# Two attention branches change places, and the first unit is prepared partly inside the branch

## The chip, the cores and the metric

The kernel runs on one core of one Trainium2 chip. The metric is the device time of one execution in microseconds; the number that counts is the median of several runs.

## The reference

Sliding-window attention with sink keys, then a mixture of eight experts whose gate is balanced in 8 rounds of row and column scaling, then one more layer. Everything is float32 in the reference; the last layer's weights come as float64.

```python
# attention: q, k, v are (2, 8, 768, 64); n_sink = 4, window = 128
scores = q @ k.T / sqrt(D)
keep = (key < n_sink) | ((0 <= query - key) & (query - key < window))
a = softmax(where(keep, scores, -1e9))          # + 1e-09 in the denominator
x = (a @ v) as (1536, 512)                      # heads side by side
# mixture: w_gate (512, 8), w1 (8, 512, 1024), w2 (8, 1024, 512)
P = exp(x @ w_gate - max)
for _ in range(8):
    P /= P.sum(1) + 1e-9;  P /= P.sum(0) + 1e-9;  P *= N / E
x = sum over e of P[:, e] * (relu(x @ w1[e]) @ w2[e])
# last layer: w_in (512, 2048), w_out (2048, 512)
h = x @ w_in
out = (h - tanh(h)) @ w_out
```

n_sink and window are inputs of the run, not constants.

## The kernel before

The order of all work is written out by hand (the scheduler is set to manual), so each engine does its instructions in the order in which the code issues them. Products run on float32 values that are split into a high and a low part (`split`, `split_hi`: ACT casts the high part at L58 or L63, DVE subtracts it at L59 or L64 to get the low one), three products for one.

`run` first issues the loads of the keys and queries of units 0 and 1 (`load_unit`, L198, on SP's queue). A unit is two heads of one batch, so there are 8 units, each with 6 tiles of 128 queries. Then it builds the mask material: `far` and `col` on POOL, finished on DVE from the two run-time numbers, `flag_i` (L134: 1 where n_sink is at most 32 and window is between 1 and 128) and three bias tiles: `b0` (L142) for the first tile of queries, `b1` (L160, L161, and a memset) for the second, `b2` (L164 to L166) for the others. SP then issues the loads of the first four weight pieces (`stage_next`, L517, 512 KB each).

Behind that come the first products. `keep_busy` (L187) issues products of zeros that nothing reads, in order to keep PE's clock up. `prep` prepares a third of a unit: four transposes on PE (L209) into one PSUM bank, the casts on ACT (L63) into `kT` and `qT`, and then the subtractions on DVE (L64); it is a generator with three steps, so the caller decides what lies between them. For unit 0, third `part` has the tiles 2*part and 2*part + 1 of keys and of queries. For third 0 POOL also copies the sink keys into their slots (L224). Before the branch all three thirds of unit 0 are prepared, in three PSUM banks of their own, with 8, 4 and 4 zero products between them; `b1` and `b2` are made on DVE in between.

Then every engine reads the flag into a register and branches. If the flag is 1, `attention_narrow` runs; otherwise `attention_any`, a longer program for any window, which is compiled into the kernel but not run with these inputs. The arms lie in memory in the order in which the code has them: code up to the branch, the arm for a true condition, the arm of `Else`, the code behind the join.

`attention_narrow` is a loop over 48 steps t (unit u, tile i) and five more to drain it. Step t issues, in this order: scores of tile t on PE (`qk`, L267); on DVE the bias with the maximum (`soft1`, `araw`, L284), together with the end of the sums of step t - 1 (L278, L289); in the first three steps four zero products; the scaling of the probabilities of step t - 1 on DVE (`soft3`, L306); what earlier steps left in the list `later` (above all DVE subtractions, L64); in the odd tiles the four transposes of a third of the next unit into pool `ps_t`; the transposes of the probabilities of step t - 2 (`a_transpose`, L320 and L325), also into `ps_t`, with a copy on ACT; the exponentials on ACT (`soft2`, L297); then the casts of the third, whose subtractions are put into `later`; and the products with v of step t - 3 (`pv`, L356, from tile 1 on). `ps_t` has two buffers of one PSUM bank each.

Behind the join `moe` runs: `g1` (L662) and `g2` (L669) are the products of the experts and of the last layer, and the gate's steps lie among the first of them.

## Time and profile before

| | |
|---|---|
| median of 3 runs | 1465.67 us |
| fastest run | 1465.48 us |
| span of the profiled execution, first to last instruction | 1464.2 us |
| PE busy with products | 1443.6 us, 99% of the span |
| DVE, ACT, POOL busy | 864.4, 451.3, 141.7 us |
| chain that ended last: PE, DVE, "issue", ACT | 82%, 12%, 3%, 3% |
| last attention product ends | 122.3 us after the span's start |

The span leaves out what lies around the first and the last instruction, 1.5 us against the median. The chain that ended last is followed back from the last instruction to whatever released it; "issue" in it is time in which the engine waited for nothing that the profile shows. A product's end is modelled, so durations of neighbouring products overlap; the distance between their starts is the better measure.

### The profile page before, as it was taken

What the parts mean: (1) busy time and instruction counts of PE and PEld (TensorE: products, weight loads), DVE (VectorE), ACT (ScalarE), POOL (GpSimd) and SP (SyncE); (2) the same over time, 40 slices, a digit from 0 to 9 for tenths busy, and PEclk for the clock granted to TensorE, in tenths of its full rate; (3) what the DMA queues carried; (4) which work ended last, traced back from release to release, by engine and by line L of the source; (5) the groups of instructions that cost most, each with busy time, mean ns of one, the idle gap of its engine ahead of it and who ended that gap; (6) DMA issues with size and microseconds to landing.
All of it is one profiled execution on the core that took longest, in us unless ns stands there. A gap on an engine that the chain in (4) does not pass through costs nothing.

```text
span 1464.2 us, 17440 instructions
## 1 busy us (share of the span) xinstructions
PE 1443.6 (99%) x6731; PEld 1171.0 (80%) x6731; DVE 864.4 (59%) x1810; ACT 451.3 (31%) x864; POOL 141.7 (10%) x127
## 2 busy tenths in 40 slices
PE   8999999999999999999999999999999999998998
PEld 6666888888888888888888888888888878787887
DVE  6893233466356446625653563465352289999997
ACT  6994212200211210022112102210211256665553
POOL 1110000000000000000000000000000135346431
PEclk9999999999999999999999999999999999999999
DMA  7341000321121031112112211221220011000011
GB/s 166 84 125 37 29 1 12 106 66 48 49 96 52 28 101 65 58 41 93 54 37 86 79 53 34 94 65 36 73 76 4 23 36 43 15 30 29 0 44 44
DMA packets 91674, 81.05 MB, mean 55 GB/s; under 512 B 42816, under 2 KB 71744, under 8 KB 91584
## 3 DMA queue, kind: packets, MB, share of 16 engines
q1 hardware_dynamic: 91296, 79.86, 18.0%
q8 instruction: 55, 0.90, 0.2%
q14 instruction: 35, 0.29, 0.1%
q10 hardware_dynamic: 288, 0.00, 0.0%
HBM read 68.31 MB, written 11.53 MB: 55 GB/s over the span
## 4 chain that ended last, share of the span: by engine, by line
PE 82%; DVE 12%; issue 3%; ACT 3%; DMA 0%; POOL 0%; SPq 0%; DVEq 0%; ACTq 0%
PE p L662 40%; PE p L669 39%; DVE y L764 3%; ACT an L297 2%; DVE mk L758 1%; DVE y L761 1%; DVE y L759 1%; DVE y L763 1%; DVE araw L284 1%; DVE an L306 1%; PE pt L325 1%; DVE kT L64 0%; PE pg L609 0%; PE sc L267 0%; ACT at L326 0%
## 5 line engine op out<-in xcount | busy, mean ns | idle before, releaser
L669 PE MATMUL p<-w2p,h 128*128 128x512 f32 x2880 | 669.1, 390 | 8.2 <-ACT h L769 4.9
L669 PEld LDWEIGHTS p<-w2p,h 128*128 128x128 f32 x2880 | 539.3, 188 | 122.8 <-POOL h L770 5.2
L662 PE MATMUL p<-xh,w1p 128*128 128x512 f32 x1920 | 608.5, 392 | 2.2 <-issue 2.2
L662 PEld LDWEIGHTS p<-xh,w1p 128*128 128x128 f32 x1920 | 362.6, 189 | 78.3 <-issue 3.1
L662 PE MATMUL p<-xl,w1p 128*128 128x512 f32 x960 | 375.4, 391 | 0.0
L694 ACT ACTIVATE h<-p 128x512 fp32r<-128x512 f32 x192 | 114.8, 598 | 791.9 <-PE p L662 787.4
L695 DVE SCALAR_TENSOR_TENSOR h<-p,h 128x512 fp32r<-128x512 f32 x192 | 132.5, 690 | 259.6 <-ACT h L694 259.3
L662 PEld LDWEIGHTS p<-xl,w1p 128*128 128x128 f32 x960 | 181.4, 189 | 37.5
L683 DVE SCALAR_TENSOR_TENSOR acc<-p,prob,acc 128x512 f32<-128x512 f32 x84 | 63.0, 750 | 206.1 <-PE p L669 206.1
L59 POOL TENSOR_TENSOR w1p<-stage,w1p 128x1024 fp32r<-128x1024 f32 x8 | 22.0, 2747 | 1041.3 <-ACT w1p L58 1041.3
L770 POOL TENSOR_TENSOR h<-y,h 128x512 fp32r<-128x512 f32 x47 | 81.6, 1735 | 145.4 <-DVE th L762 141.9
L764 DVE COPY_PREDICATED y<-mk,th 128x512 f32<-128x512 uint8 x48 | 84.1, 1751 | 1.7
L760 ACT ACTIVATE tq<-tq,kst 128x512 f32<-128x512 f32 x48 | 34.8, 725 | 78.1 <-DVE y L759 78.1
L297 ACT ACTIVATE an<-araw,nmax 128x288 f32<-128x288 f32 (+1 forms) x96 | 48.7, 514 | 2.7 <-DVE nmax L284 2.1
L758 DVE TENSOR_SCALAR mk<-tq 128x512 uint8<-128x512 f32 x48 | 43.1, 898 | 2.1 <-ACT tq L755 2.1
L59 DVE TENSOR_TENSOR w2p<-stage,w2p 128x1024 fp32r<-128x1024 f32 x32 | 39.2, 1225 | 7.9 <-ACT w2p L58 7.9
L58 ACT CAST w2p<-stage 128x1024 fp32r<-128x1024 f32 x40 | 41.7, 1043 | 0.0
L284 DVE CUSTOM_DVE_ANT_0 araw<-sc,bias 128x288 f32<-128x288 f32 (+1 forms) x96 | 39.7, 414 | 0.0
L267 PE MATMUL sc<-kT,qT 64*128 64x288 f32 (+1 forms) x288 | 36.9, 330 | 0.4 <-DVE qT L64 0.3
L755 ACT ACTIVATE tq<-p 128x512 f32<-128x512 f32 x48 | 28.7, 597 | 27.2 <-PE p L662 27.2
L267 PEld LDWEIGHTS sc<-kT,qT 64*128 64x128 f32 x288 | 23.4, 185 | 15.3 <-issue 14.6
L58 ACT CAST w1p<-stage 128x1024 fp32r<-128x1024 f32 x36 | 35.6, 1047 | 0.0
(129 smaller groups left out, 953.9 us busy)
## 6 DMA issues: line engine op xcount, KB each, us to landing
stage<-in_moe_w_dram SPq DMA_DIRECT2D x64, 512.0 KB, 3.5
n<-in_moe_w_in_dram SPq DMA_DIRECT2D x32, 256.0 KB, 2.8
n<-in_moe_w_out_dram SPq DMA_DIRECT2D x32, 256.0 KB, 2.7
wf_in<-n SPq DMA_DIRECT2D x32, 128.0 KB, 1.7
wf_out<-n SPq DMA_DIRECT2D x32, 128.0 KB, 1.7
stage<-wf_in SPq DMA_DIRECT2D x8, 512.0 KB, 3.2
stage<-wf_out SPq DMA_DIRECT2D x8, 512.0 KB, 3.6
v<-in_v_dram SPq DMA_DIRECT2D x16, 192.0 KB, 2.5
```

What stands on the lines that cost most here:

```text
L58: self.nc.scalar.copy(out=hi, in_=src)
L59: (engine or self.nc.vector).tensor_tensor(out=lo, in0=src, in1=hi.bitcast(F32), op=ALU.subtract)
L267: nc.tensor.matmul(sc[t][h][:, :n], lhsT=self.qT[u % 2][rows, zq, i * P : (i + 1) * P], rhs=self.kT[u % 2][rows, zk, c0 : c0 + n], start=m ...
L297: nc.scalar.activation(out=an[t][:, h, :n], in_=araw[t][:, h, :n], func=AF.Exp, bias=nmax[t][:, h : h + 1], scale=-1.0, accum_out=ssum[t][ ...
L662: nc.tensor.matmul(ps, lhsT=wt[:, zw, kk, cols], rhs=xx[:, kk, tok], start=m == 0, stop=m == 3 * KD - 1)
L669: nc.tensor.matmul(ps, lhsT=ht[:, zh, n * P : (n + 1) * P], rhs=ws[j // 2][:, zw, j % 2, :], start=start and m == 0, stop=stop and m == last,)
L683: V.scalar_tensor_tensor(out=acc[n], in0=ps, scalar=prob[:, n, e : e + 1], in1=acc[n], op0=ALU.mult, op1=ALU.add)
L694: nc.scalar.activation(out=h[j][:, 0], in_=ps, func=AF.Relu)
L695: V.scalar_tensor_tensor(out=h[j][:, 1], in0=ps, scalar=0.0, in1=h[j][:, 0].bitcast(F32), op0=ALU.max, op1=ALU.subtract)
L758: V.tensor_scalar(out=mk, in0=tq, scalar1=TAN_T2, scalar2=None, op0=ALU.is_ge)
L764: V.copy_predicated(y, mk, th)
L770: engine.tensor_tensor(out=ht[:, 1], in0=y, in1=ht[:, 0].bitcast(F32), op=ALU.subtract)
```

## The change

The condition of the branch is turned round: the arm for `flag == 0` comes first and is `attention_any`, the `Else` arm is `attention_narrow`. Before the branch only third 0 of unit 0 is prepared, with 8 and 4 zero products, in 2 PSUM banks instead of 4. The other two thirds are prepared in steps 0 and 2 of the loop of `attention_narrow`, in `ps_t`; `b1` is made in step 0 and `b2` in step 1. The rest of the diff takes out comments and docstrings.

```diff
+            self.far, self.col = far, col
             with ExitStack() as early:
-                pools = [early.enter_context(tc.tile_pool(name=f"ps_w{i}", bufs=1, space=PSUM)) for i in range(4)]
+                pools = [early.enter_context(tc.tile_pool(name=f"ps_w{i}", bufs=1, space=PSUM)) for i in range(2)]
                 busy = pools[0].tile([P, 512], F32, name="busy")
-                first = [self.prep(0, part, pools[1 + part], "m") for part in range(3)]
+                first = self.prep(0, 0, pools[1], "m")
                 self.keep_busy(busy, 8)
-                next(first[0])
+                next(first)
                 self.keep_busy(busy, 4)
-                next(first[1])
-                next(first[0])
-                next(first[0])
-                self.keep_busy(busy, 4)
-                next(first[2])
-                V.tensor_tensor(out=b1[:, :P], in0=far[:, 0], in1=col, op=ALU.max)
-                V.tensor_copy(out=b1[:, TW:], in_=far[:, 1])
-                for part in (1, 1, 2, 2):
-                    next(first[part])
-                V.tensor_copy(out=b2[:, :P], in_=far[:, 0])
-                V.tensor_copy(out=b2[:, P:TW], in_=col[:, :SK])
-                V.tensor_copy(out=b2[:, TW:], in_=far[:, 1])
+                next(first)
+                next(first)
...
-            with tc.If(flag == 1) as cond:
+            with tc.If(flag == 0) as cond:
                 with ExitStack() as c1:
-                    self.attention_narrow(c1)
+                    self.attention_any(c1)
             with cond.Else():
                 with ExitStack() as c2:
-                    self.attention_any(c2)
+                    self.attention_narrow(c2)
...
             if t <= T:
                 soft1(t)
+            if t == 0:
+                b0, b1, b2 = self.bias
+                nc.vector.tensor_tensor(out=b1[:, :P], in0=self.far[:, 0], in1=self.col, op=ALU.max)
+                nc.vector.tensor_copy(out=b1[:, TW:], in_=self.far[:, 1])
+            elif t == 1:
+                nc.vector.tensor_copy(out=b2[:, :P], in_=self.far[:, 0])
+                nc.vector.tensor_copy(out=b2[:, P:TW], in_=self.col[:, :SK])
+                nc.vector.tensor_copy(out=b2[:, TW:], in_=self.far[:, 1])
             if t < 3:
                 self.keep_busy(ps_k.tile([P, 512], F32, tag="k", name=self.nm("busy")), 4)
...
             if t < T and u + 1 < units and i % 2 == 1:
                 pr = self.prep(u + 1, i // 2, ps_t, "t")
                 next(pr)
+            elif t in (0, 2):
+                pr = self.prep(0, 1 + t // 2, ps_t, "t")
+                next(pr)
```

## Rows read from the trace of the kernel before

**Rows 1.** Chain of waits over the whole span: start us, us, what.

```profile
by line: PE p L662 39.8%; PE p L669 39.1%; DVE y L764 2.9%; issue 2.8%; ACT an L297 1.6%; DVE mk L758 1.3%; DVE y L761 1.3%; DVE y L759 1.2%; DVE y L763 1.2%; DVE araw L284 0.8%; DVE an L306 0.7%; PE pt L325 0.7%; DVE kT L64 0.4%; PE pg L60
...
179.18 5.49 PE p L662 x24
```

**Rows 2.** Chain of waits, 110 to 160 us, at the join.

```profile
122.36 2.22 issue
124.58 8.56 PE p L662 x24
```

**Rows 3.** Windows at the join: length, engines' busy time, PEclk, DMA share, GB/s.

```profile
122.40:123.80 1.40, 0.00 (x0) 0.00 (x0) 0.69 (x1) 0.57 (x1) 0.60 (x3) 1.00 0.15 14
...
124.58:130.60 6.02, 6.02 (x14) 4.78 (x15) 0.19 (x1) 0.71 (x2) 0.00 (x0) 0.50 0.02 5
```

**Rows 4.** Timeline at the join: start us, us, instruction, [idle before, releaser].

```profile
121.22 1.12 PE L368 MATMUL px<-ats,vS 64*128 64x512 f32 x2
...
123.00 0.69 DVE L64 TENSOR_TENSOR xl<-px,xh 128x512 fp32r<-128x512 f32 x1 [3.59 <-ACT xh L63]
...
125.95 0.19 DVE L59 TENSOR_TENSOR wgs<-wg,wgs 128x32 fp32r<-128x32 f32 x1 [2.26 <-ACT wgs L58]
```

**Rows 5.** DMA queues, 121 to 126 us: packets, MB, share of 16 engines.

```profile
q8 instruction: 2, 0.03, 2.4%
q14 instruction: 3, 0.02, 1.8%
```

**Rows 6.** Timeline up to the branch, 0 to 12 us.

```profile
6.04 1.17 PE L187 MATMUL busy<-idle 128*128 128x512 f32 x4
6.28 0.16 DVE L134 TENSOR_TENSOR flag_i<-ok 128x1 int32<-128x1 f32 x1
7.48 0.41 DVE L64 TENSOR_TENSOR qT<-m,qT 128x256 fp32r<-128x256 f32 x1
8.27 0.34 POOL L245 MEMSET vS<- 64x128 f32 x2 [0.33 <-issue]
8.29 0.41 PE L209 MATMUL m<-ident,raw_q 128*128 128x128 f32 x2 [0.78 <-DMA raw_q<-in_q_dram]
```

**Rows 7.** DMA queues, 0 to 15 us.

```profile
q1 hardware_dynamic: 7861, 3.10, 88.9%
```

**Rows 8.** Timeline of the first attention steps, PE and DVE.

```profile
10.32 0.55 PE L267 MATMUL sc<-kT,qT 64*128 64x128 f32 x6 [0.25 <-DVE qT L64]
13.23 0.46 DVE L284 CUSTOM_DVE_ANT_0 araw<-sc,bias 128x288 f32<-128x288 f32 x1
13.78 0.60 PE L209 MATMUL m<-ident,raw_k 128*128 128x128 f32 x4
14.06 0.47 DVE L306 TENSOR_SCALAR an<-an,ssum 128x128 f32<-128x128 f32 x2
14.31 0.67 PE L267 MATMUL sc<-kT,qT 64*128 64x288 f32 x6
15.01 0.46 DVE L284 CUSTOM_DVE_ANT_0 araw<-sc,bias 128x288 f32<-128x288 f32 x1
16.40 0.68 DVE L64 TENSOR_TENSOR kT<-m,kT 128x512 fp32r<-128x512 f32 x1
17.34 0.60 PE L325 MATMUL pt<-ident,an 128*128 128x128 f32 x4
17.88 0.45 DVE L284 CUSTOM_DVE_ANT_0 araw<-sc,bias 128x288 f32<-128x288 f32 x1
19.71 0.45 DVE L284 CUSTOM_DVE_ANT_0 araw<-sc,bias 128x288 f32<-128x288 f32 x1
21.89 0.66 PE L325 MATMUL pt<-ident,an 128*128 128x128 f32 x4 [0.29 <-DVE qT L64]
```

**Rows 9.** Windows on DVE, subtractions of a third, then the last bias tile.

```profile
10.79:11.46 0.67, 0.67 (x3) 1.00 1.11 303
11.46:11.90 0.44, 0.44 (x5) 1.00 1.11 340
```

## The prediction

> **What bounds the kernel now.** I read the chain of waits first. Its summary by line gives 39.8% of the span to the products of L662 alone, and a stretch of them at full speed looks like 24 products in 5.49 us [rows 1]; once these products run, little else ends last. A change ahead of them is therefore worth what it moves their start. That start is set by the attention stage and by one hole behind it: the last attention product ends, the chain shows 2.22 us of "issue" (PE waits for nothing that the profile knows of), and the next 24 products take 8.56 us instead of 5.49 [rows 2]. [...] So the join of the two branches costs 2.22 + 3.07 = 5.3 us today.

> What the hole is shows in the timeline there. PE starts its last attention group at 121.22 and the next product at 124.58, 3.36 later; DVE starts its last attention subtraction at 123.00 and its next instruction at 125.95, 2.95 later [rows 4]. Pauses of about 3 us on both, at different moments, are hardly one engine waiting for another. In the same five microseconds the instruction queues move 2 and 3 packets [rows 5]: the engines jump from the end of the short-window arm over the whole any-window arm, and the code behind it has to be fetched. At the start there is no such jump: the arm that runs is the one that lies next, and POOL's idle time at that branch is 0.33 us [rows 6], the price of reading the flag and falling through.

> **The change, part by part.**

> *The join.* The short-window arm now lies last, next to the code that follows, so its end needs no far jump. Removed: the 2.22 us (0.1 us is left, for a short branch) and, if PE goes on without a hole, the slow clock behind it, 8.56 - 5.49 = 3.07 us [rows 1, 2]. Gain 5.2 us. Its bounds are 2.1 (the clock falls all the same, since the last attention steps are thin) and 5.3.

> *The branch.* The far jump is now at the start, over the any-window arm. By the loops of that arm PE skips 2 x (48 + 6 x 116) = 1488 products, each with its weight load; DVE and ACT skip some hundreds of instructions, SP and POOL a few dozen. The price of such a jump lies between PE's hole of 2.22 and 3.36 us; I take DVE's 2.95, as that instruction stands alone and is timed from its start [rows 2, 4]. When do the engines jump? The flag is written at 6.28 + 0.16 = 6.44. PE's four zero products of 6.04 end at 7.21 [rows 6]; with 0.5 us to read the flag (POOL's 0.33, rounded up) PE jumps at 6.95, while they still run, and goes on at 9.9. DVE's last subtraction of the first third starts at 7.48 [rows 6]; with the flag it jumps at 8.0 and goes on at 10.95. But the loads of this time take 88.9% of the DMA engines over the first 15 us [rows 7], where the join had them nearly idle. I add 0.3 us (bounds: 0, and 3, a doubling): **PE at 10.2, DVE at 11.2**. Before, the first scores started at 10.32 [rows 8].

> [...]

> If SP paid 3 us too, its first load of v would start that much later, but v is first read in step 4 of the loop, which itself moves by more.

> *What the pause takes the place of.* Until 10.32 PE prepared the other two thirds (the last queries landed at 8.29 [rows 6]), ACT cast them, DVE subtracted and made two bias tiles. Ahead of the branch go away 8 transposes, 4 zero products, 4 casts, 4 subtractions and 5 bias instructions. All but the zero products come back inside the loop; no DMA moves. The bias tile of step 0 costs nothing: DVE makes it while PE does that step's zero products. What costs is 0.67 us for two subtractions of a third and 0.44 for the bias tile of step 1 [rows 9].

> *PE's clock.* PE idles from 7.21 to 10.2. At the join the clock fell 1.4 us into such a hole and came back after 6.0 us of products [rows 3]. I take the same: half speed from 10.2 to about 16.2. Bound below: no fall.

> *The first steps* (durations from [rows 8]). From 10.2 at half speed: first scores 1.0 us (0.55 at full), four zero products 1.7 (0.43 each, 14 in 6.02 us [rows 3]), four transposes of the second third 1.1, the second scores 1.3 up to the first head. DVE's second pair of araw starts at **15.3** instead of 13.23, +2.1. At full clock the same line gives 13.1, -0.1. From araw DVE needs 14.06 + 0.47 - 13.23 = 1.30 us to the end of the scaling, then the new 1.11 us of bias and subtractions, on which the third scores wait; from scores to araw it is 15.01 - 14.31 = 0.70, and 0.1 for the event. So 3.2 us instead of 1.78: araw of step 2 comes **+3.5** late.

> *A wait that is new.* In the loop the thirds live in ps_t, two banks that the transposes of the probabilities use too. Units are prepared in odd steps, so that in the next step one bank stays free; now preparations run in steps 0, 1, 2 and 3. A preparation's bank comes free with its subtractions, which DVE does a step later. In step 2 the new third holds one bank, and the probabilities' transposes need the other, which DVE frees at the end of its own step 2; in step 3 it is the same. PE's next scores are queued behind these transposes, DVE's next araw waits for the scores. (The wait exists today with a step's slack: the transposes of 21.89 wait 0.29 us for DVE [rows 8].) Step 2 to 3: araw and scaling 16.40 - 15.01 = 1.39, subtraction 0.68, two transposes 0.4, scores 0.67, events 0.1: 3.25 instead of 17.88 - 15.01 = 2.87, +0.4. Step 3 to 4: 1.39 + 0.67 + 0.60 + 0.67 + 0.1 = 3.4 instead of 19.71 - 17.88 = 1.83, +1.6. From there the steps are the old ones. **Loss 5.5 us**; below that 1.35 (full clock, another bank), above it what the fetch takes more.

> **Sum.** 5.5 lost at the start, 5.2 won at the join: +0.3. The profiled span of 1464.2 becomes 1464.5; with the 1.5 us between that span and the median of the runs, 1466.0.

> **The rivals.**

> A. The above: two effects of one size. 1466.0, by itself 1465.0 to 1467.5. Chance 0.44.

> B. The clock holds at the start, since PE was busy up to the hole, while the join's hole came after thin work. Loss 5.5 - 2.15 = 3.35, net -1.85: 1463.8. Against it: 3 us idle, twice what the clock bore at the join. 0.17.

> C. Slower: the code is fetched among the loads and takes 6 us instead of 3. All behind it moves by 3 us more: net +3.3, 1469.0. From a fetch of 3 us on the change loses. For it: the 88.9%; against it: code has a queue of its own. 0.13.

> D. Slower, since the change doesn't do what it says: the hole at the join isn't the far jump, or a fetch comes there anyway. Nothing is won, 5.5 lost: 1471.2. Against it: PE and DVE pause at different times for one length. 0.09.

> E. The banks cost nothing, as ACT is what steps 2 to 4 wait for anyway. Loss 3.5, net -1.7: 1464.0. 0.13. Together with B: loss 1.35, net -3.85, 1461.8, 0.04.

> **How the numbers follow.** The forecast is A. 1462.3 to 1469.6 holds A, B, C and E (0.87) and leaves out D and the pair of B and E. 2% is 29 us, about what a measurement of this kernel can tell from no change; the largest case, D, is 5.5 us, and 2% would need a fetch of over 30 us. So faster 0.01, same 0.98, slower 0.01.

> **What would show it.** At the join: the first L662 product within 0.3 us of the last attention product, the clock at 1.00, 24 products in 5.5 us; a gap of 2 us there is D. At the start: a packet on an instruction queue before 10 us; PE idle from 7.2 to about 10.2, a much later end being C; the granted clock of 10 to 16 us at 0.50, and 1.00 being B. In the loop: transposes of steps 2 and 3 that wait for DVE's subtractions, the first araw of step 4 near 25.2 instead of 19.71, and the last attention group near 121.2 + 5.5 = 126.7; without these waits it is E. The forecast is wrong altogether if the products from the join to the end don't take the time they took before.

## The result

The changed kernel takes 1472.64 us (median, 1472.17 to 1474.54), the kernel before 1465.62 us beside it. Single runs far outside the rest (1595.86 us for the kernel before, 2403.75 for the loop alone below) are left out of all ratios. The ratio is 1.0052, with a 95% interval of 1.0037 to 1.0067: slower, clear of noise, though far within 2%. The forecast was 1466.0 in a range of 1462.3 to 1469.6. The span of the profiled execution is 1470.6 us instead of 1464.2, so 6.4 us have to be found.

The page of the changed kernel counts lines of its own file: its scores are L258, its transposes of the probabilities L311 and L316, its expert products L664 and L671.

The join did what was forecast. The chain of waits of the changed kernel, 118 to 165 us (start us, us, what; to be compared with [rows 2]), and the start of the last attention group in the timeline (to be compared with [rows 4]):

```profile
132.61 1.05 PE px L359 x2
133.66 5.67 PE p L664 x24
...
132.54 1.12 PE L359 MATMUL px<-ats,vS 64*128 64x512 f32 x2
```

There is no hole any more, and 24 products take 5.67 us instead of 8.56. From the start of the last attention group (121.22 before [rows 4], 132.54 now) to the end of these products it was 124.58 + 8.56 - 121.22 = 11.92 us [rows 2, 4] and is 133.66 + 5.67 - 132.54 = 6.79: 5.1 won, against 5.2 forecast.

But that last group starts 11.3 us later than before, where 5.5 were forecast. 11.3 - 5.1 = 6.2 is the loss of the span but for 0.2 us. All of the error lies at the start. The chain of waits there, 0 to 40 us:

```profile
7.33 4.64 issue
11.96 0.91 PE sc L258 x6
12.87 2.00 PE busy L178 x4
14.87 0.85 PE m L200 x4
15.73 0.78 PE sc L258 x3
16.50 0.92 issue
17.43 0.45 PE sc L258 x3
```

PE is without work for 4.64 us at the branch, and then a second time for 0.92, in the middle of the second scores: three of their six products are done, the next three wait for nothing that the profile knows of. The instruction queues, 6 to 10 us:

```profile
q8 instruction: 1, 0.02, 2.0%
q14 instruction: 2, 0.02, 1.4%
```

So code is fetched at the start now, among the loads (225 GB/s from 6.0 to 9.6 us); before, neither queue has a packet in the first 15 us. In windows of 0.1 us the packet on q8 comes at 9.0, 2.9 us before PE goes on, and its next at 15.1, 2.3 us before PE goes on again. What follows in the loop shows the timeline of the first steps (start us, us, instruction, [idle before, releaser]; to be compared with [rows 8]):

```profile
17.96 0.46 DVE L275 CUSTOM_DVE_ANT_0 araw<-sc,bias 128x288 f32<-128x288 f32 x1 [3.48 <-PE sc L258]
...
20.77 0.46 DVE L275 CUSTOM_DVE_ANT_0 araw<-sc,bias 128x288 f32<-128x288 f32 x1 [0.27 <-PE sc L258]
...
22.98 0.41 PE L311 MATMUL pt<-ident,an 128*128 128x128 f32 x2 [0.69 <-DVE kT L64]
...
23.43 0.37 ACT L312 COPY at<-pt 128x256 f32<-128x256 f32 x1 [3.36 <-PE pt L311]
23.70 0.54 ACT L288 ACTIVATE an<-araw,nmax 128x288 f32<-128x288 f32 x1
...
24.87 0.17 DVE L269 TENSOR_SCALAR ssum<-ssum 128x2 f32<-128x2 f32 x1 [2.04 <-ACT an L288]
24.95 0.45 DVE L275 CUSTOM_DVE_ANT_0 araw<-sc,bias 128x288 f32<-128x288 f32 x1
...
27.13 1.12 PE L316 MATMUL pt<-ident,an 128*128 128x128 f32 x4 [2.57 <-DVE qT L64]
...
29.95 0.17 DVE L269 TENSOR_SCALAR ssum<-ssum 128x2 f32<-128x2 f32 x1 [2.87 <-ACT an L288]
30.02 0.45 DVE L275 CUSTOM_DVE_ANT_0 araw<-sc,bias 128x288 f32<-128x288 f32 x1
```

Here the wait for the banks is in the trace as forecast: the transposes of steps 2 and 3 wait for DVE's subtractions (0.69 and 2.57 us). What the reader should see beside it is ACT: its copy of the transposed probabilities starts at 23.43, and the exponentials of the step, whose input DVE had finished at 21.7, come behind that copy in ACT's order. DVE then waits 2.04 us for them, and in the next step 2.87 us in the same way. The windows of PE (length, busy, granted clock, DMA share, GB/s):

```profile
9.60:16.20 6.60, 4.24 (x17) 0.50 1.04 311
16.40:26.60 10.20, 6.29 (x38) 1.00 0.79 178
26.80:33.40 6.60, 6.27 (x29) 0.50 0.00 1
33.60:40.00 6.40, 6.40 (x59) 1.00 0.01 3
```

PE's clock falls twice: in the hole, as forecast, and again at about 26.7, in the 2.57 us in which PE waits for DVE. The four transposes behind that wait take 1.12 us, not 0.60.

The start of the first araw of a step, from the DVE timelines of all these kernels, gives the account by steps (us; the loop alone from its second run):

| step | before | changed | swap only | loop only | own bank |
|---|---|---|---|---|---|
| 1 | 13.23 | 17.96 | 23.54 | 10.84 | 18.43 |
| 2 | 15.01 | 20.77 | 26.40 | 13.65 | 21.82 |
| 3 | 17.88 | 24.95 | 29.27 | 17.84 | 25.12 |
| 4 | 19.71 | 30.02 | 31.11 | 22.91 | 27.73 |
| 7 | 26.36 | 37.74 | 37.75 | 31.43 | 35.80 |

Changed against before: 4.73 late at step 1, then 1.03, 1.31 and 3.24 more in the next three steps, 1.07 more up to step 7, together 11.38. Behind that the distance stays.

### The profile page after: what moved, and what is told of

Its sections match the earlier page's. It is cut to its first block, busy times and chain, and to the rows that moved or that the text cites. A ratio compares the mean times of both kernels' runs of the same rounds, so it can differ in the third digit from the quotient of the medians.

```text
span 1470.6 us, 17424 instructions
## 1 busy us (share of the span) xinstructions
PE 1445.0 (98%) x6727; PEld 1171.7 (80%) x6727; DVE 865.2 (59%) x1810; ACT 450.9 (31%) x864; POOL 141.6 (10%) x127
## 4 chain that ended last, share of the span: by engine, by line
PE 83%; DVE 11%; issue 3%; ACT 2%; POOL 0%; DVEq 0%; ACTq 0%
PE p L664 39%; PE p L671 39%; DVE y L766 3%; ACT an L288 1%; DVE y L763 1%; DVE mk L760 1%; DVE y L765 1%; DVE y L761 1%; PE pt L316 1%; DVE araw L275 1%; PE sc L258 1%; DVE an L297 1%; PE px L347 1%; PE m L200 1%; PE busy L178 0%
## 5 line engine op out<-in xcount | busy, mean ns | idle before, releaser
L671 PE MATMUL p<-w2p,h 128*128 128x512 f32 x2880 | 669.4, 390 | 8.5 <-ACT h L771 4.8
L671 PEld LDWEIGHTS p<-w2p,h 128*128 128x128 f32 x2880 | 539.5, 188 | 122.8 <-POOL h L772 5.3
L664 PE MATMUL p<-xh,w1p 128*128 128x512 f32 x1920 | 606.1, 390 | 0.0
L664 PEld LDWEIGHTS p<-xh,w1p 128*128 128x128 f32 x1920 | 361.2, 188 | 75.4 <-issue 0.8
L664 PE MATMUL p<-xl,w1p 128*128 128x512 f32 x960 | 374.0, 390 | 0.0
L664 PEld LDWEIGHTS p<-xl,w1p 128*128 128x128 f32 x960 | 180.6, 188 | 37.2
L258 PE MATMUL sc<-kT,qT 64*128 64x288 f32 (+1 forms) x288 | 38.5, 343 | 5.8 <-issue 5.6
L258 PEld LDWEIGHTS sc<-kT,qT 64*128 64x128 f32 x288 | 24.4, 195 | 21.9 <-issue 21.2
```

The lines of the kernel that those rows point to most:

```text
L258: nc.tensor.matmul(sc[t][h][:, :n], lhsT=self.qT[u % 2][rows, zq, i * P : (i + 1) * P], rhs=self.kT[u % 2][rows, zk, c0 : c0 + n], start=m ...
L664: nc.tensor.matmul(ps, lhsT=wt[:, zw, kk, cols], rhs=xx[:, kk, tok], start=m == 0, stop=m == 3 * KD - 1)
L671: nc.tensor.matmul(ps, lhsT=ht[:, zh, n * P : (n + 1) * P], rhs=ws[j // 2][:, zw, j % 2, :], start=start and m == 0, stop=stop and m == last,)
```

## The experiments

Theory T, formed from these rows: the start loses by code that is fetched among the loads, by a second packet of code that is fetched right behind the first, and by the waits in steps 2 to 4, with the second fall of the clock. Rival R: all of it is the fetch of code, that of DVE and ACT included, and the banks cost nothing.

**The swap alone and the loop alone.** The two halves of the change, each by itself. The swap alone, in the kernel before:

```diff
-            with tc.If(flag == 1) as cond:
+            with tc.If(flag == 0) as cond:
                 with ExitStack() as c1:
-                    self.attention_narrow(c1)
+                    self.attention_any(c1)
```

(and the other arm in the Else). The loop alone is the changed kernel with these lines put back.

> The arms change places, but all three thirds and the bias tiles are still made ahead of the branch. Theory T (the 11.3 us that the changed kernel loses at its start are a fetch of 5 us among the loads, a second small one behind it, and waits for two PSUM banks in steps 2 to 4, with a second fall of PE's clock): the join wins its 5.2 us here too; PE jumps at about 10.1 and goes on at about 15, the steps behind that are as long as before. With 4 to 5 us of hole and the slow clock behind it some 6 us are lost, net +1 to +2: 1466.5 to 1468. Rival R (the steps of the loop are late because the arms' code, that of DVE and ACT too, keeps being fetched; the banks cost nothing): steps 2 to 4 are stretched here as well, and the time is that of the changed kernel, 1471 to 1473.

> The arms stay as they were; only the preparation of the other two thirds and of two bias tiles goes into the loop. Theory T: no hole at the branch, the join's hole and slow clock stay; the steps 2 to 4 are stretched by the wait for the banks, +4 to +6 us against before, less the 1 us by which the loop starts earlier: 1468.5 to 1471. Rival R (banks cost nothing): 1465 to 1467, steps 2 to 4 within 0.5 us each of what they were.

Measured: the swap alone 1472.22 us against 1465.03 before on that chip, ratio 1.005 (1.0033 to 1.0067); the loop alone 1469.53, ratio 1.0028 (1.0018 to 1.0037). Each half loses by itself. The swap alone cost 4 to 6 us more than T had said, and the timeline shows why:

```profile
14.28 0.55 PE L267 MATMUL sc<-kT,qT 64*128 64x128 f32 x6 [4.25 <-issue]
...
20.32 2.08 PE L187 MATMUL busy<-idle 128*128 128x512 f32 x4 [5.49 <-issue]
```

Two holes, 4.25 and 5.49 us, with six products between them. The second is the one that is 0.92 us long in the changed kernel. The swap wins at the join all the same, where the hole is closed:

```profile
132.59 1.05 PE px L368 x2
133.64 5.68 PE p L662 x24
```

The clock, too, went another way than in the changed kernel: it held through the whole first hole, 10.03 to 14.28 us, and fell only between 14.5 and 15.0, behind six more products (windows of PE; it waits again from 14.83):

```profile
14.00:14.50 0.50, 0.22 (x4) 1.00 1.07 363
14.50:15.00 0.50, 0.33 (x6) 0.85 1.12 365
15.00:15.50 0.50, 0.00 (x0) 0.50 1.12 363
```

R's number came out, but not its mechanism: from step 2 on the steps of this kernel take 2.87, 1.84 and so on, what they took before (2.87 and 1.83, [rows 8]). Code is late twice, and then no more. The table's "swap only" has all of its 11.4 us by step 2. The losses of the two halves, 7.2 and 4.5 us, do not add up to the 7.0 of the whole, since the second hole is 5.49 us long in one and 0.92 in the other.

The loop alone was run once more for a profile:

> The loop's part alone once more, for a profile: steps 2 to 3 and 3 to 4 at 4.2 and 5.1 us with no jump near by; PE waits there for DVE's subtractions, and the clock falls in the wait. Rival R: 2.9 and 1.8 us.

It took 1470.32 us. No far jump is near its first steps, and yet they take 2.81, 4.19 and 5.07 us, to 0.02 us those of the changed kernel (2.81, 4.18, 5.07):

```profile
15.87 0.41 PE L311 MATMUL pt<-ident,an 128*128 128x128 f32 x2 [0.68 <-DVE kT L64]
...
20.02 1.12 PE L316 MATMUL pt<-ident,an 128*128 128x128 f32 x4 [2.56 <-DVE qT L64]
```

On q8, whose packets stand ahead of PE's returns, none lands between 5 and 23 us here, on q14 one. R falls. The loop enters 2.4 us earlier (step 1 at 10.84) and is 3.2 us late at step 4, 5.6 us in three steps: 1.0 is the longer step 1, with DVE's new work, and 4.6 are the two steps with the waits. The chain of waits at its join still has the old hole:

```profile
127.68 2.31 issue
```

**A bank of its own.**

```diff
-                pr = self.prep(0, 1 + t // 2, ps_t, "t")
+                pr = self.prep(0, 1 + t // 2, ps_x, "x4")
```

> The changed kernel, with the two thirds that are prepared in the loop put into the bank of px that is not used before step 4, not into ps_t. Theory T: steps 2 to 3 and 3 to 4 take 2.9 and about 2.6 us where the changed kernel has 4.2 and 5.1, PE's clock doesn't fall a second time; 4 to 5 us less than the changed kernel: 1467.5 to 1468.5. Rival R: no difference, 1472.6.

Measured 1471.19, ratio 1.0038 (1.0024 to 1.0052) to before. The steps came near what was expected, 3.30 and 2.61 us (expected 2.9 and 2.6) instead of 4.18 and 5.07, so the bank is what these two waits were. The time did not: 6.2 us above before on that chip, where the changed kernel was 7.0 above, and the intervals of the two ratios overlap. At the last attention group 2.0 us of the gain are left (130.54 against 132.54). Where the 3.3 us went that these two steps won:

```profile
11.00:21.00 10.00, 7.84 (x28) 0.50 1.01 279
21.50:27.50 6.00, 4.64 (x36) 1.00 0.60 129
28.00:31.00 3.00, 3.00 (x16) 0.50 0.00 0
```

These are windows of PE again. The clock stayed low to 21 us instead of 16.3. The edit is not shown to be the cause of that: already ahead of the branch, and so ahead of anything that it touches, the four zero products took 1.77 us in this execution instead of 1.18, and the clock fell at 10.9 instead of 9.5. The clock fell once more at 27.9 us, 1.0 us behind the end of another wait, which the timeline of this kernel shows:

```profile
26.97 0.73 PE L258 MATMUL sc<-kT,qT 64*128 64x288 f32 x4 [0.94 <-DVE kT L64]
```

That is the score of step 4 itself, which needs the third that was prepared in step 2. With the banks out of the way the data is late. So this run shows what the two waits were; how much time they are worth by themselves it does not show, as the clock differs as well.

**The fetch among the loads.** The swap alone, with the other loads held back; the small writes make them wait for DVE's first araw:

```diff
+            if t == 0:
+                for s in self.stage:
+                    nc.vector.memset(s[:, :1], 0.0)
+                for n in "kq":
+                    nc.vector.memset(self.qk_raw[(n, 1)].rearrange("p a b d -> p (a b d)")[:, ::D], 0.0)
+                self.load_unit(1)
+                for _ in range(4):
+                    self.stage_next()
+                load_v(0)
```

(and taken out at their old places).

> The swap alone (as e1_swap_only), with the loads of unit 1, of the four weight pieces and of the first v held back until DVE has done its first araw, by eight small writes ahead of them (so the loop behind it is later; only the two holes count here). Theory T (fetches are slow because they share the DMA engines with the loads): PE's two holes shrink from 4.25 and 5.49 us to about 3.0 and at most 3. Rival (fetching the arm takes that long wherever it is done): 4.3 and 5.5 again.

```profile
11.86 0.55 PE L264 MATMUL sc<-kT,qT 64*128 64x128 f32 x6 [2.36 <-issue]
15.15 2.07 PE L184 MATMUL busy<-idle 128*128 128x512 f32 x4 [2.75 <-issue]
```

The same two holes at the same two places, 2.36 and 2.75 us instead of 4.25 and 5.49. So about half of each goes with the loads. The quiet figures, at a DMA share of 0.00 to 0.14 in the windows of the two holes (0.87 to 1.43 in the first hole of the swap alone), are near that of the join before the change, 2.22 us at a share of 0.15 [rows 2, 3]. Where the loads' share lies shows the start of q8's packet, in windows of 0.1 us: 1.5 us into the first hole of the swap alone (11.5), and 0.2 us ahead of that hole here (9.3); at the second, 2.6 us into it (17.4) and 0.2 (12.6). From the packet to PE's return it is 2.8 and 2.6 us, then 2.9 and 2.6, so most of the time is lost ahead of the packet. This is one execution. Its time, 1471.89 us, says little, as the loads that the loop needs come later.

**Where the arm lies.** The changed kernel, with zero products added to the arm that is never run, so that nothing but the place of the other arm moves:

```diff
                 self.split(self.xh[:, :, tok], self.xl[:, :, tok], pt)
+        self.keep_busy(ps_s.tile([P, 1024], F32, tag="sc", name=self.nm("gpad"))[:, :512], 18)
```

> The changed kernel with 18 zero products put at the end of the any-window arm, which is not run: only the place of the short-window arm in memory moves, by 36 PE instructions. Theory T (PE's second hole, 0.92 us at 16.5 behind the 17th product, is the border to a block of code that is not there yet): that hole disappears, the first stays at 4.6 us; 1471 to 1472, 1 us less than the changed kernel. Rival (PE waits there for something in the loop): the hole stays, 1472.6.

Measured 1478.22, ratio 1.0088 (1.0071 to 1.0105): 13.2 us above before on that chip instead of 7.0, by instructions that nobody executes. The second hole was gone, but the first had taken it in:

```profile
17.80 0.90 PE L258 MATMUL sc<-kT,qT 64*128 64x128 f32 x6 [9.96 <-issue]
```

and q8, whose packets stood ahead of PE's returns so far, has one packet before this first score and one shortly ahead of it (windows 6 to 9 and 15 to 18 us):

```profile
q8 instruction: 1, 0.02, 2.9%
...
q8 instruction: 1, 0.02, 1.9%
```

Two packets, and one return of PE. That fits an arm that now starts just ahead of the end of a packet of code, not behind it as I had meant, but this is an estimate from the lengths of the holes: where a packet ends no run shows. A second test of this is the same with 22 products:

> The changed kernel with 22 zero products in the arm that isn't run, instead of 18. With 18 the first hole became 9.96 us long and two blocks of code came ahead of the first score; with 40 PE instructions more ahead of the arm (e5_zero_hole) there was one block only and no second hole. Theory T (what counts is the distance from the arm's first instruction to the next border of a block): 44 instructions move the border past the start, first hole 4.6 us as in the changed kernel, no second: 1471 to 1472. Rival (more code to skip makes the fetch longer): a hole of 10 us again, 1478.

```profile
11.67 0.90 PE L258 MATMUL sc<-kT,qT 64*128 64x128 f32 x6 [4.44 <-issue]
...
15.36 0.94 PE L258 MATMUL sc<-kT,qT 64*128 64x288 f32 x6
```

1471.24 us, ratio 1.0041 (1.0026 to 1.0056): one hole, no second, the second scores in one piece, araw of step 1 at 16.43 instead of 17.96. The second packet on q8 comes here too, at 15.2 us, but PE has work up to then and beyond. Eight instructions of PE's code between these two kernels are worth 7 us, 6.3 of them at step 1 (22.71 with 18 products). What the traces show of the fetch is this: a packet of about 16 KB on q8 (0.90 MB in 55 packets; the expectations call it a block) comes ahead of each of PE's returns, and the second hole changes when the arm is moved (0.92 us in the changed kernel, merged with the first at 18 products, none at 22).

**Zeros over the hole.** The kernel with a bank of its own, and

```diff
-                self.keep_busy(busy, 4)
+                self.keep_busy(busy, 24)
```

> The run with a bank of its own for the two thirds, and 24 zero products in place of 4 ahead of the branch. They move the arm by 40 PE instructions, too. Theory T: PE's sequencer hands the zeros out early, so the jump is not late; the zeros run to about 11.3, PE goes on at 12 at a clock of 1.00, and as the arm now starts just behind a border between two blocks of code, the second small hole (1.20 us at 16.5) is gone. Second pair of araw at about 14.8 instead of 18.4, clock no lower than 1.00 up to 25 us; 3.5 to 5 us less than e3_own_bank, 1466 to 1467.5. Rival (the jump waits until the zeros have left PE's queue): PE goes on at 15 to 16, no gain, 1471.

Measured 1467.2, ratio 1.0015 (1.0005 to 1.0024), 4.0 us less than without the zeros (1.0038, 1.0024 to 1.0052). The zeros end at 12.29, the first score runs at 13.23, and the windows of PE show no fall:

```profile
6.00:12.30 6.30, 6.29 (x26) 1.00 1.22 249
12.30:13.23 0.93, 0.00 (x1) 1.00 1.06 341
13.23:30.00 16.77, 15.13 (x111) 1.00 0.69 171
```

The score is 1.3 us later than in the changed kernel, and q8's packet comes at 10.3 us instead of 9.0, so the zeros delayed the jump somewhat; the rival had a part of the truth. The gain mixes the clock and the second hole, which is not there in this run (1.20 us with the own bank alone).

**What beats both.** The join's other half, the clock, can be had without the swap. In the kernel before, behind the loop:

```diff
+        self.keep_busy(ps_k.tile([P, 512], F32, tag="k", name=self.nm("busy")), 10)
```

> The kernel before, with ten products of zeros behind the last attention product, ahead of the jump. Theory T (the join's hole is a fetch of about 3 us that PE's sequencer starts once it has handed out its last product, and 3.07 us of the join are the clock alone): the zeros run during the fetch, the clock stays at 1.00, the next 24 products take 5.5 us instead of 8.56, the first of them starts where it did: 1462.6. Rival (the sequencer jumps only when the zeros are nearly done): the first product comes up to 2.2 us later, 1462.6 to 1464.8.

> The zero tail once more, with more rounds: 2 to 3 us below before, the interval of its ratio below 1.

First 1463.48 against 1465.03, ratio 0.9991 (0.9981 to 1.0); with more rounds 1463.37 against 1465.07, ratio 0.9988 (0.9979 to 0.9997), less than the 2 to 3 us expected. It has the lowest median of all, if by little; the first interval touches 1, the second ends just below. The chain of waits at its join (second run):

```profile
121.37 1.05 PE px L368 x2
122.43 2.49 PE busy L187 x10
124.92 5.60 PE p L663 x24
```

The zeros lie in the hole, the first product starts 0.3 us later than it did (124.58, [rows 2]), and 24 of them take 5.60 us instead of 8.56: 2.7 us won by this view, 1.7 by the medians.

Last, the early loop, meant to be without its waits, together with this tail: the arms as before, the second third in step 0 in the bank of px, the last in step 1 in that of `ps_k`, and no zero products in steps 1 and 2.

> Built from what the runs showed: the arms as before (no jump among the loads), the loop entered with the first third alone; the second third is made in step 0 in the free bank of px, the last in step 1 in the bank of ps_k, instead of the zero products of steps 1 and 2, so that no step waits for a bank of ps_t; ten zero products behind the last attention product. Theory T: second araw at about 10.8 (13.23 before), steps of 2.8, 3.0 and 1.9 us, the fifth at 18.5 (19.71 before), no fall of the clock at the start or at the join: 1.2 + 2.9 us less than before on the same chip, about 1461. Rival (DVE and ACT, with two thirds in step 1, become late and give the head start back): no less than the run with the zero tail, 2 us below before.

Measured 1463.71 against 1465.07, ratio 0.999 (0.9981 to 0.9999): no better than the tail alone, as the rival said. The second araw came at 10.92 and step 4's at 19.39 where 18.5 was expected. The windows of PE:

```profile
6.00:16.00 10.00, 7.86 (x52) 1.00 1.18 282
16.50:23.00 6.50, 6.49 (x27) 0.50 0.99 210
```

The zero products of steps 1 and 2 were gone, PE waited, the last time 1.02 us up to 16.51 for DVE's subtraction (in the bank of `ps_t` that a third of unit 1 still takes), and the clock fell to 0.50 at about 16.3. From step 4 to 7 this kernel takes 8.23 us instead of 6.65, and its last attention group starts 1.2 us later than before. That is where the head start went; whether the zeros alone would have kept it wasn't tried.

## Why the prediction was wrong, point by point

The forecast failed at one place, the loss at the start: 11.3 us where the sum has 5.5. Two of its terms were too small there, the price of the jump and the wait for the banks, and one was missing, the second packet of code. The number lies beyond the range and nearest to rival D's 1471.2, which is chance, since D's mechanism, a join that wins nothing, did not come.

- **The join** was right, place, mechanism and size: 5.1 us against 5.2, the hole closed, the clock at 1.00. Of the 0.1 us put down for a short branch the chain shows nothing: the attention ends and the products start at 133.66. Rival D is out. That the old hole was a far jump is shown by the swap alone, which closes it, and the loop alone, which leaves it (2.31 us).
- **The price of the jump** was the first wrong term: PE at 11.96, not 10.2, +1.76 us. I took a duration from a place with a DMA share of 0.15 ([rows 3], 2.95 us) and added 0.3 for a place with 88.9% [rows 7]; quiet loads give back about half of such a hole (2.36 against 4.25, the swap alone). Rival C had this mechanism, with too low a chance. By the same sum, with the jump at 6.95 as it was assumed, 2.1 us were measured in place of the 0.3 (11.96 - 9.9). Most of what the loads add lies ahead of q8's packet, as the quiet run shows; what the packet waits for, no run shows.
- **The second packet of code** is the step that was missing. The sum had one fetch for a jump. The changed kernel has two packets on q8, at 9.0 and 15.1 us, and PE goes on behind the second 5.5 us after it did behind the first (11.96 and 17.43), in the swap alone 6.0 (14.28 and 20.32). What the second cost went with how much work PE had in between: 0.92 us in the changed kernel, with 4.5 us of products, 5.49 in the swap alone, with 0.55, all of it with 18 products of padding (one hole of 9.96), none with 22. No row of the kernel before shows it at the start. At the join it was on record: [rows 5] has two packets on q8. One comes at 122.0 us, just ahead of the hole (122.36, [rows 2]), the other at 125.2, when PE already has its products again, and so it cost nothing that I could see there.
- **The clock at the start** fell and came back as forecast, 0.50 from about 9.5 to 16.3 (forecast 10.2 to 16.2). Rival B is out for this kernel. But the level was right and the two times were luck: the fall came 2.2 us into the hole, not 1.4, and the return 4.3 us after PE's, not 6.0. In the swap alone the clock held through the whole first hole (4.25 us) and fell only behind the six products that followed. The line at full clock has a slip too: 0.55 + 0.86 + 0.60 + 0.67 us from 10.2 give 12.9, not 13.1, which makes B's loss 0.2 us smaller and leaves the forecast as it is.
- **Step 1 to 2** took 2.81 us, forecast 3.2. The 0.1 us for an event, here and in the next sum, was an estimate; in the changed kernel it is 0.04 to 0.15 us from the end of what was waited for to the next start (20.73 to 20.77, 22.83 to 22.98).
- **The wait for the banks** was right in place and wrong in size: 4.18 and 5.07 us, forecast 3.25 and 3.4. I followed PE's queue from the transposes to the scores and stopped there. The wait also holds ACT, whose copy waits for the transposes and whose exponentials are queued behind that copy; DVE's next sums need them (2.04 and 2.87 us of idle time). And PE's clock fell a second time, to 0.50, in its wait of 2.57 us. Rival E (banks cost nothing) is refuted by the loop alone and by the own bank.
- **"From there the steps are the old ones"** was wrong by 1.07 us, with the clock at 0.50 to 33.4.

In sum: araw of step 1 at +4.73 instead of +2.1 (1.76 fetch, 0.92 second packet), the next three steps +5.58 instead of +3.4, then +1.07. Together that is the error at the last attention group but for 0.1 us, 11.3 against 5.5. And the 29 us that the prediction calls about what a measurement can tell are far too many: the interval of this ratio is 4.4 us wide, and a loss of 7.0 is clear of noise.

## What to carry to other kernels

Here a far branch cost one fetch of code and, in five of the seven kernels with the swap, a part or all of a second, which changed with the place of the arm (0.92 us, back to back with the first at 18 zero products in the other arm, none at 22); look for the second packet in the instruction queue's row. Price the fetch with one measured under the DMA load of the place it is moved to, and look at the clock that the hole takes down. When a shared bank makes one engine wait, follow every engine that has an instruction behind that wait, to the next value that the first engine needs. And where half of a hole's price is the slow clock behind it, as at this join, a few products of nothing inside the hole can be cheaper than moving it (1.7 us won here, where the move lost 7.0).
